# A linear-attention and two-layer MLP kernel: accumulator tiles by bank, another end, another order, diagonals moved to GpSimd, smaller PE tiles in the state update

## The chip, the cores and the metric

One core of a Trainium2 chip. The metric is the device time in microseconds (us) of one execution. All tensors are fp32 in HBM.

## The reference, cut to what matters

```python
# r, k, v, w: (batch 4, heads 8, seq 768, dim 48); u: (8, 48)
for t in range(S):                       # linear attention, a state of 48x48 for each head
    cur = einsum('bhd,bhe->bhde', u * k[t], v[t])
    y[t] = einsum('bhd,bhde->bhe', r[t], state + cur)
    state = w[t][..., None] * state + einsum('bhd,bhe->bhde', k[t], v[t])
x = y as (3072 tokens, 384)
h = x @ w_in                             # 384 -> 2048
g = where(h > 0, h, exp(min(h, 0)) - 1)  # ELU
out = g @ w_out                          # 2048 -> 384
```

## The kernel before, in words

The sequence is cut into 24 **units** and 6 **chunks** of 512 tokens (`NC`, `N`), four units to a chunk. Units 0 to 3 ("whole") hold 128 steps of one batch, units 4 to 23 ("pair") 64 steps of two batches. The weights come packed and are turned on the chip into a high part (fp32r) and a low part; for the first six of the 16 slices of d_ff (`K32 = 6`) chunk 0 uses an fp32 copy instead.

One **unit** is these tasks: loads of w, k and r, v (and of r and k by token, `rk`, where GpSimd makes the diagonal); two scans on VectorE (`e_scan` L430, `g_scan` L440) for the decays; `hats` L445 scales k and r; the diagonal term r*k*u; `spread`, which lays the diagonal out in the tile `am`; on TensorE `score` (L510 transposes, L518 products, and for pair units the first `state_part` at L497); `mask` L528 puts the scores above the diagonal into `am` (VectorE); on TensorE `value` (second `state_part`, then am times v at L497, then the state update kt times v at L553); last the copies `xf`, `xh`, `xl` (L576, L569, L573) that hand 128 columns of x to the MLP and `update` L581 or L583 of the state. A whole unit's first copy is `xf` on ScalarE. The diagonal of units 0 to 7 (`DIAG`) is made by four narrow products on TensorE (`diag_pe` L469) after `r_k_rows` L464 on VectorE; that of units 8 to 23 by two products on GpSimd (L452, L455) and a reduction on VectorE (L459).

One **step** of the MLP is one chunk with one slice f: `g1` makes h by 9 fp32r products of 512 columns (L261; 3 fp32 ones at L257 for the copy), `r1`, `r2` on ScalarE, `stt` on VectorE make the ELU, `gh` on ScalarE and `gl` on VectorE split it, `g2` adds 9 products of 512 columns (L295; L292 for fp32) into the accumulator, three output banks of 512 columns. In chunk 0 the first six steps, in chunk 1 the first four (`FH = (6, 4)`) are done in two halves of 256 columns, so that the first half needs only the chunk's first two units. The accumulator is one tile of three banks (L238). At the end of a chunk ScalarE copies the banks out (`out` L302). The last step of the last chunk is split (L749): bank 0, bank 1, and bank 2 in two halves, each followed by its copy (`end` L308) and its store.

The order of all instructions is made when the kernel is built: `Plan.order` (L115) is a list scheduler over tasks with costs (`COST`), due times (`BEGINS`) and offsets to them (`NUDGE`); each engine then runs its own list in order, with semaphores between engines. Until the time `WARM_END` gaps of the plan on TensorE are filled with products of the identity that nobody reads (`warm` L404).

Of the kernel before, what the change touches and what calls it, by code (L numbers as in the profile page):

```python
# [8 lines left out]
F32 = mybir.dt.float32  # L9
# [27 lines left out]
FH = (6, 4)  # L37
# [23 lines left out]
COST = dict(es=1.2, gs=1.5, pc=0.2, pd=0.9, md=0.2, spa=2.0, spd=0.62, rh=0.62, hat=1.15, rk=0.48, rku=0.48, prk=1.2, prku=1.35, dg=0.5, mk=0.65, mk0=1.2, up=0.48, sc=0.48, xl=0.48,  # L61
            cand=0.56, cv=0.96, wl=0.88, stt=0.62, gl=0.64, fl=0.95, kt=0.53, xh=0.48, a=0.92, sg=2.0, la=0.95, wh=0.82, r1=0.6, r2=0.62, gh=0.62,
            sp=1.95, s=1.6, s0=1.6, s2=1.1, v=1.92, v0=1.6, v2=1.3, g=2.05, g32=2.65, out=0.6)
LAT = 0.06
# [12 lines left out]
DIAG = ["PE"] * 8 + ["POOL"] * 16  # L77
# [6 lines left out]
NUDGE = dict(a={5: -43.25, 8: -22.5, 15: 19.5},  # L84
             cc={5: -29.75, 6: -3.25, 8: 20.75, 11: 8},
             es={1: -8, 3: 25.5, 7: 9.25, 9: 4.75, 16: -17.5},
             g1={2: -0.75, 14: -22, 16: -9.25, 18: -25, 23: -2.25, 24: -6, 25: 30, 34: -0.75, 37: -5.25, 38: -10.75, 42: -10.75, 43: -28.5, 44: 6, 45: 22, 53: 1.75, 57: -5, 60: 8.5, 64: -3.5, 66: -26.25, 68: -19, 76: -26.5, 80: 2.75, 91: 1.5, 104: 4},
             g2={13: 11.5, 18: -40.75, 19: -29, 20: 4, 32: 12.75, 35: 21, 38: 6.25, 47: 2.75, 50: 7.75, 51: 22, 55: 10.25, 61: -25.75, 67: 44.75, 70: 54},
             raw={0: -6},
             rh={0: -1.75, 1: -6.5, 4: 7.5, 8: -2.5, 13: 25.5, 18: -25},  # L90
             s={2: 9, 5: 8, 6: 16.25, 7: 27, 20: 10.5},
             sp={4: -6.5, 5: 1.5, 6: -6.25, 8: 8.75, 10: 15, 11: -0.75, 17: 27.25},
             v={1: 10.5, 2: -32.5, 15: -11.25, 23: -2.5},
             wl={10: 1.25, 11: 8.5, 13: -21})
# [3 lines left out]
class Plan:  # L98
# [16 lines left out]
    def order(self):  # L115
# [31 lines left out]
        for k in ts:  # L147
            if not count[k]:
                ready[ts[k]["eng"]].append(k)
        events, now, order = [], 0.0, []  # L150
        while len(order) < len(ts):
            moved = False
            for e in ready:
# [34 lines left out]
                busy[e] = end  # L188
# [16 lines left out]
            for end, k in sorted(x for x in events if x[0] <= now + 1e-9):  # L205
# [25 lines left out]
def mlp(nc, w_h, w_l, ps_acc, ps_h, ml, gp, po, dst, last=False, w_f=()):  # L231
# [49 lines left out]
    def g2(s, only=None):  # L281
        f, lo, hi = s["f"], s["lo"], s["hi"]
        for m in range(NK):
            parts = 2 if (s["final"] and m == NK - 1 and last) else 1
            for q in range(parts):
                if only not in (None, (m, q)):
                    continue
                s_ = slice(q * (hi - lo) // parts, (q + 1) * (hi - lo) // parts)
                a_ = cut(s, accs()[m]) if s.get("wide") else accs()[m][:, lo + s_.start:lo + s_.stop]
                first, final = s["first"], s["final"] and q == parts - 1  # L290
                if f < len(w_f):
                    nc.tensor.matmul(a_, w_f[f][:, 1, m], fold(s, s["m"][:, s_]), start=first, stop=final)  # L292
                    continue
                for n, (w, g) in enumerate(((w_h, s["gh"]), (w_h, s["gl"]), (w_l, s["gh"]))):
                    nc.tensor.matmul(a_, w[f][:, 1, m], fold(s, g[:, s_]), start=(first and n == 0), stop=(final and n == 2))  # L295
# [8 lines left out]
    def end(m, q):  # L304
        parts = 2 if m == NK - 1 else 1
        s_ = slice(q * N // parts, (q + 1) * N // parts)
        t = po.tile([P, N // parts], F32, tag=("wraw1", "wraw", "wg")[m], name="o", bufs=m or 1)
        (nc.scalar.copy if m + q in (0, 2) else nc.vector.tensor_copy)(t, acc[m][:, s_])  # L308
        (nc.scalar if m + q == 2 else nc.sync).dma_start(dst[m * P:(m + 1) * P, s_], t)
# [4 lines left out]
    return dict(g1=g1, r1=r1, r2=r2, stt=stt, gh=gh, gl=gl, g2=g2, out=out, store=store, end=end)  # L314
# [3 lines left out]
def rwkv_elu_kernel(ctx, tc, wkr, rk, vp, u, uz, gkrw, gv, gu, wraw, out):  # L318
# [69 lines left out]
    def pair(u_):  # L388
        if u_["i"] in SPARE:
            return spare()[:, 0:2]  # L390
        return ps_a.tile([P, 2, N], F32, tag="pa", name="pa", bufs=1)
# [4 lines left out]
    def spare():  # L396
        if not held:
            held.append(ps_acc.tile([P, NK, N], F32, tag="acc", name="acc"))
        return held[0]

    def warm(n):
        pw = spare()[:, 2, 0:P]
# [103 lines left out]
    def score(u_):  # L506
# [6 lines left out]
        u_["pa"] = pa = both[:, :, 0:n].rearrange("t q (p s) -> t q p s", p=NP)  # L513
        for p in range(NP):
            for lo in range(0, C, u_["L"]):
                for q in range(2):
                    rs, ts = slice(64 * q, 64 * q + D), slice(lo, lo + u_["L"])
                    nc.tensor.matmul(pa[ts, 1 - q, p], u_["k"][rs, p, ts], u_["r"][rs, p, ts], start=True, stop=True)  # L518
# [19 lines left out]
    def value(u_):  # L538
# [8 lines left out]
        if u_["last"]:  # L547
            return
# [393 lines left out]
```

## Time and profile before

| what | us |
|---|---|
| median of 3 runs (516.56 to 518.71) | 516.65 |
| the profiled execution, its own time | 519.32 |
| its span, from the first to the last instruction | 517.6 |
| TensorE busy (98%) | 506.4 |
| VectorE busy (65%) | 335.3 |
| ScalarE busy (53%) | 272.9 |
| GpSimd busy (16%) | 85.1 |

The profiled execution lies 1.7 us above its span and 2.7 us above the median. A matmul's row shows a start and a modelled length that runs into the next one; what it costs in a stream is the distance from start to start. An fp32 product is two records, so "x32" at L553 is 16 products.

### The profile page before, as it was taken

To read this page: it belongs to the slowest core of one execution; us is meant where nothing else is said; L and a number is where in the kernel's file an instruction comes from. 1 tells how busy PE (TensorE), PEld (TensorE's weight loads), DVE (VectorE), ACT (ScalarE), POOL (GpSimd) and SP (SyncE) were. 2 spreads that over 40 slices of the span, in tenths; PEclk is the share of its full clock that TensorE was granted. 3 is DMA by queue.
4 is the path that set the end of the run, shared out by engine and by line. 5 is a ranking of instruction groups with operands and counts; after the bars stand their busy time and mean duration, and the time that the engine had idled before them with its cause. 6 is when DMAs were issued, how large, how long until landed. Compare 5 with 4: busy or idle time off the path is not lost.

```text
span 517.6 us, 13928 instructions
## 1 busy us (share of the span) xinstructions
PE 506.4 (98%) x6095; PEld 419.1 (81%) x6095; DVE 335.3 (65%) x475; ACT 272.9 (53%) x534; POOL 85.1 (16%) x85
## 2 busy tenths in 40 slices
PE   8999999999999999999999999999999999999993
PEld 7898888888988888888878888888887877888882
DVE  7799999997789733878524687524788433423331
ACT  4678776857555533656534644425555343634441
POOL 2000000003265500145120034300342100000000
PEclk9799999999999999999999999999999999999997
DMA  8967523402953210533172214312311000100001
GB/s 253 330 230 230 167 83 139 157 3 74 255 155 95 69 53 3 161 107 99 37 229 57 80 50 136 107 59 58 108 49 60 2 3 1 62 0 2 0 1 66
DMA packets 18307, 49.53 MB, mean 96 GB/s; under 512 B 2240, under 2 KB 2624, under 8 KB 18240
## 3 DMA queue, kind: packets, MB, share of 16 engines
q1 hardware_dynamic: 18096, 48.44, 30.3%
q8 instruction: 50, 0.82, 0.7%
q14 instruction: 17, 0.14, 0.1%
q10 hardware_dynamic: 144, 0.13, 0.1%
HBM read 43.85 MB, written 4.72 MB: 94 GB/s over the span
## 4 chain that ended last, share of the span: by engine, by line
PE 96%; ACT 1%; DVE 1%; DMA 1%; issue 0%; DVEq 0%; ACTq 0%
PE acc L295 37%; PE ph L261 37%; PE pa L497 6%; PE acc L292 3%; PE ph L257 3%; PE pa L518 3%; PE pa L553 3%; PE pb L510 2%; PE pb L469 1%; PE acc L404 1%; DMA w<-in_wkr_dram 1%; ACT am L479 0%; PE acc L518 0%; DVE eg L430 0%; DVE eg L440 0%; DVE o L308 0%
## 5 line engine op out<-in xcount | busy, mean ns | idle before, releaser
L271 DVE SCALAR_TENSOR_TENSOR m<-m,ph 128x512 f32<-128x512 f32 (+1 forms) x106 | 66.8, 633 | 89.7 <-ACT m L268 89.3
L265 ACT ACTIVATE m<-ph 128x512 f32<-128x512 f32 (+1 forms) x106 | 59.0, 557 | 99.1 <-PE ph L261 83.7
L295 PE MATMUL acc<-gh,w_l 128*128 128x512 f32 (+1 forms) x283 | 107.5, 380 | 0.0
L261 PE MATMUL ph<-xh,w_l 128*128 128x512 f32 (+1 forms) x282 | 107.4, 381 | 0.0
L279 DVE TENSOR_TENSOR gl<-m,gh 128x512 fp32r<-128x512 f32 (+1 forms) x94 | 65.1, 698 | 47.4 <-ACT gh L275 47.2
L275 ACT CAST gh<-m 128x512 fp32r<-128x512 f32 (+1 forms) x94 | 56.4, 600 | 69.2 <-PE acc L295 40.7
L295 PE MATMUL acc<-gh,w_h 128*128 128x512 f32 (+1 forms) x192 | 74.3, 387 | 0.0
L261 PE MATMUL ph<-xh,w_h 128*128 128x512 f32 (+1 forms) x192 | 74.1, 386 | 0.0
L295 PE MATMUL acc<-gl,w_h 128*128 128x512 f32 (+1 forms) x192 | 72.5, 377 | 0.0
L261 PE MATMUL ph<-xl,w_h 128*128 128x512 f32 (+1 forms) x192 | 72.3, 377 | 0.0
L268 ACT ACTIVATE m<-m 128x512 f32<-128x512 f32 (+1 forms) x106 | 62.5, 591 | 3.0
L295 PEld LDWEIGHTS acc<-gh,w_l 128*128 128x128 f32 x283 | 53.2, 188 | 10.5
L261 PEld LDWEIGHTS ph<-xh,w_l 128*128 128x128 f32 x282 | 53.0, 188 | 10.5
L490 POOL TENSOR_SCALAR_AFFINE_SELECT am<-md 64x512 f32<-64x512 f32 x32 | 32.9, 1027 | 169.9 <-DVE md L459 158.0
L295 PEld LDWEIGHTS acc<-gh,w_h 128*128 128x128 f32 x192 | 36.1, 188 | 7.5
L261 PEld LDWEIGHTS ph<-xh,w_h 128*128 128x128 f32 x192 | 36.1, 188 | 7.1
L261 PEld LDWEIGHTS ph<-xl,w_h 128*128 128x128 f32 x192 | 36.2, 188 | 6.1
L295 PEld LDWEIGHTS acc<-gl,w_h 128*128 128x128 f32 x192 | 36.1, 188 | 6.0
L295 PE MATMUL acc<-gh,w_g 128*128 128x512 f32 (+1 forms) x91 | 36.0, 396 | 1.5 <-DVE o L308 0.8
L261 PE MATMUL ph<-xh,w_g 128*128 128x512 f32 x90 | 36.1, 401 | 0.0
L295 PE MATMUL acc<-gl,w_g 128*128 128x512 f32 (+1 forms) x91 | 35.2, 387 | 0.0
L261 PE MATMUL ph<-xl,w_g 128*128 128x512 f32 x90 | 35.1, 390 | 0.0
(101 smaller groups left out, 718.3 us busy)
## 6 DMA issues: line engine op xcount, KB each, us to landing
wraw<-in_wraw_dram SPq DMA_DIRECT2D x16, 768.0 KB, 5.7
k<-in_wkr_dram SPq DMA_DIRECT2D x24, 448.0 KB, 5.6
v<-in_vp_dram SPq DMA_DIRECT2D x24, 256.0 KB, 6.0
rk<-in_rk_dram SPq DMA_DIRECT2D x16, 384.0 KB, 4.0
w<-in_wkr_dram SPq DMA_DIRECT2D x24, 227.9 KB, 3.9
out_dram<-o SPq DMA_DIRECT2D x17, 256.0 KB, 2.3
wx<-in_wkr_dram SPq DMA_DIRECT2D x8, 227.9 KB, 2.6
ub<-in_u_dram SPq DMA_DIRECT2D x1, 192.0 KB, 6.3
```

The source lines that it names most:

```text
L257: nc.tensor.matmul(ph, w_f[f][:, 0, k], x_[2][:, k], start=(k == 0), stop=(k == NK - 1))
L261: nc.tensor.matmul(ph, w[f][:, 0, k], y[:, k], start=(k == n == 0), stop=(k == NK - 1 and n == 2))
L265: act(s["m"], s["ph"], AF.Relu, scale=-1.0)
L268: act(s["m"], s["m"], AF.Exp, scale=-1.0)
L271: stt_(s["m"], s["m"], -1.0, s["ph"], ALU.add, ALU.max)
L275: nc.scalar.copy(s["gh"], s["m"])
L279: nc.vector.tensor_tensor(s["gl"], s["m"], s["gh"].bitcast(F32), ALU.subtract)
L292: nc.tensor.matmul(a_, w_f[f][:, 1, m], fold(s, s["m"][:, s_]), start=first, stop=final)
L295: nc.tensor.matmul(a_, w[f][:, 1, m], fold(s, g[:, s_]), start=(first and n == 0), stop=(final and n == 2))
L490: nc.gpsimd.affine_select(out=am[rs].rearrange("t q p s -> t (q p) s"), in_=u_["md"][rs].rearrange("t q p -> t (q p)").unsqueeze(2).broadc ...
L497: nc.tensor.matmul(u_["py"][32 * j:32 * j + 32, h, k], l, r, **flags)
L518: nc.tensor.matmul(pa[ts, 1 - q, p], u_["k"][rs, p, ts], u_["r"][rs, p, ts], start=True, stop=True)
```

## The change

1. **One tile per output bank.** `accs` takes three tiles of one bank instead of one of three. A whole unit's scores are two tiles as well, and its `mask` two instructions.
2. **The end.** The third bank is closed two steps early and copied to SBUF (`partial`). The last two steps go to banks 0 and 1 as before; their part of bank 2 goes to other PSUM tiles, 384 columns and then 128 (`CUT`), which VectorE adds to the copy.
3. **No halves in chunk 1** (`FH`).
4. **The diagonals of units 5 to 7 on GpSimd** (`DIAG`), which adds three `rk` loads.
5. **The order searched anew**: other costs, delays and offsets of the plan. Filling products are put only ahead of the first g2.
6. **The state update of pair units by 64x32 tiles** (`WU`) instead of 64x64.

```diff
-FH = (6, 4)
+FH = (6,0)
+WU = 32
+CUT = 384
...
-LAT = 0.06
+LAT, SELF, DRAIN = 0.05, 0.035, 0.19
+NEXT = dict(PE=0.0, DVE=0.084, ACT=0.1, POOL=0.05, SP=0.0)
...
-DIAG = ["PE"] * 8 + ["POOL"] * 16
+DIAG = ['PE']*5+['POOL']*19
...
-NUDGE = dict(a={5: -43.25, 8: -22.5, 15: 19.5},
...
+NUDGE = dict(cc={6: 6.75, 7: -44.75, 10: -20.5, 14: -49.25, 15: -20},
...
     def accs():
         if not acc:
-            t = ps_acc.tile([P, NK, N], F32, tag="acc", name="acc")
-            acc.extend(t[:, m] for m in range(NK))
+            acc.extend(ps_acc.tile([P, N], F32, tag="acc%d" % m, name="acc") for m in range(NK))
         return acc
...
+    def end(m, cols=(0, N), rest=None):
+        t = po.tile([P, cols[1] - cols[0]], F32, tag=("wraw", "wraw1", "wg")[m], name="o", bufs=m or 1)
+        if rest is not None:
+            nc.vector.tensor_tensor(t, rest, box["part"][:, cols[0]:cols[1]], ALU.add)
+        else:
+            (nc.vector.tensor_copy if m else nc.scalar.copy)(t, acc[m])
+        (nc.scalar if cols[1] == N and m == 2 else nc.sync).dma_start(dst[m * P:(m + 1) * P, cols[0]:cols[1]], t)
+
+    def partial():
+        box["part"] = gp.tile([P, N], F32, tag="x2", name="part", bufs=1)
+        nc.scalar.copy(box["part"], acc[2])
...
     def mask(u_):
-        nc.vector.copy_predicated(u_["am"], above[u_["L"]], u_["pa"])
+        if u_["whole"]:
+            for q in range(2):
+                nc.vector.copy_predicated(u_["am"][:, q], above[u_["L"]][:, q], u_["pa"][q])
+        else:
+            nc.vector.copy_predicated(u_["am"], above[u_["L"]], u_["pa"])
...
+        w = 64 if whole else WU
         for p in range(NP):
-            for h, rs in enumerate(rows):
-                for z in range(2):
-                    m = 64 - 16 * z
-                    nc.tensor.matmul(u_["pu"][64 * z:64 * z + m, h, p], kt[rs, p, 64 * z:64 * z + m], v[rs, P * p + 80 * z:P * p + 80 * z + D],
+            for lo in range(0, R2, w):
+                z, m = lo // 64, min(w, R2 - lo)
+                for h, rs in enumerate(rows):
+                    nc.tensor.matmul(u_["pu"][lo:lo + m, h, p], kt[rs, p, lo:lo + m], v[rs, P * p + 80 * z:P * p + 80 * z + D],
                                      start=whole, stop=(whole or p == NP - 1))
...
+                x, y, a, b = prior, s, (0, CUT), (CUT, N)
+                add(("part",), "ACT", K["out"], fns["partial"], [("g2", n - 2)], due=due)
+                add(("g2a", 0), "PE", g * 2 / 3, lambda x=x, g2=g2: g2(x, (0, 1)), [("gl", n - 1), ("g2", n - 2)], due=due)
+                add(("g2a", 1), "PE", g / 3, lambda y=y, g2=g2: g2(y, (0,)), [("gl", n), ("g2a", 0)], due=due)
+                add(("g2a", 2), "PE", g / 3, lambda y=y, g2=g2: g2(y, (1,)), [("g2a", 1)], due=due)
+                add(("g2", n - 1), "PE", g * 2 / 3 * CUT / N, lambda x=x, y=y: rest(x, y, a, lambda: pair(units[-1])[:, 0], "a"), [("g2a", 2)], due=due)
+                add(("g2", n), "PE", g * 2 / 3 * (1 - CUT / N), lambda x=x, y=y: rest(x, y, b, single, "b"), [("g2", n - 1)], due=due)
...
-                if t["began"] < WARM_END:
+                if t["began"] < WARM_END and ("g2", 0) not in done:
```

How the order moves is shown at three places. The first is ScalarE's list around the first products of the MLP: `xf` out of `acc` is unit 1's copy, "am from ident, md" a unit's spread diagonal, "w_f from wraw" a weight slice's first conversion, "m from ph" and "m from m" are `r1` and `r2` of a step. Before:

```order
L576 COPY xf<-acc 128x6x64
L569 CAST xh<-xf 128x6x64
L473 COPY md<-pb 128x8
L596 ACTIVATE w_f<-wraw 128x768
L479 ACTIVATE am<-ident,md 128x128 x8
L265 ACTIVATE m<-ph 128x256
L268 ACTIVATE m<-m 128x256
```

Changed:

```order
L479 COPY md<-pb 128x8
L485 ACTIVATE am<-ident,md 128x128 x8
L611 ACTIVATE w_f<-wraw 128x768
L591 COPY xf<-acc 128x6x64
L584 CAST xh<-xf 128x6x64
L598 COPY st<-acc 112x4x48
L268 ACTIVATE m<-ph 128x256
```

The spread diagonal of unit 2 stood between unit 1's copy and the first step's `r1`; now it stands ahead of both.

The second place is TensorE's list at the end of `value` of a pair unit (unit 4): am times v, then the state update. Before:

```order
L497 MATMUL pa<-am,v 32x64 x32
L553 MATMUL pa<-v,kt 64x48
L553 MATMUL pa<-v,kt 48x48
L553 MATMUL pa<-v,kt 64x48
L553 MATMUL pa<-v,kt 48x48
```

Changed:

```order
L503 MATMUL pa<-am,v 32x64 x32
L568 MATMUL pa<-v,kt 32x48 x6
L568 MATMUL pa<-v,kt 16x48 x2
L568 MATMUL pa<-v,kt 32x48 x6
L568 MATMUL pa<-v,kt 16x48 x2
```

The first row and those below it now have outputs of at most 32 partitions; the products of one update are 32 where they were 16.

The third place is the end of TensorE's list, with the tiles' numbers. Before, the last nine products (`acc_5572` is the whole accumulator):

```order
L295 MATMUL acc_5572<-gh_5948,w_g_1647 128x512
L295 MATMUL acc_5572<-gl_5950,w_g_1647 128x512
L295 MATMUL acc_5572<-gh_5948,w_l_103 128x512
L295 MATMUL acc_5572<-gh_5948,w_g_1647 128x256
L295 MATMUL acc_5572<-gl_5950,w_g_1647 128x256
L295 MATMUL acc_5572<-gh_5948,w_l_103 128x256
L295 MATMUL acc_5572<-gh_5948,w_g_1647 128x256
L295 MATMUL acc_5572<-gl_5950,w_g_1647 128x256
L295 MATMUL acc_5572<-gh_5948,w_l_103 128x256
```

Changed, ten rows from the last of bank 1 on (three more of the last tile follow, with the last step's operands):

```order
L295 MATMUL acc_5757<-gh_6131,w_l_103 128x512
L295 MATMUL pa_6146<-gh_6121,w_g_1616 128x384
L295 MATMUL pa_6146<-gl_6123,w_g_1616 128x384
L295 MATMUL pa_6146<-gh_6121,w_l_103 128x384
L295 MATMUL pa_6146<-gh_6131,w_g_1635 128x384
L295 MATMUL pa_6146<-gl_6135,w_g_1635 128x384
L295 MATMUL pa_6146<-gh_6131,w_l_103 128x384
L295 MATMUL pb_6156<-gh_6121,w_g_1616 128x128
L295 MATMUL pb_6156<-gl_6123,w_g_1616 128x128
L295 MATMUL pb_6156<-gh_6121,w_l_103 128x128
```

Bank 2's products of the last two steps now stand last of all and go to tiles that no copy reads before they are done.

## Rows read from the trace of the kernel before

**Rows 1.** The page's busy time of each engine.

```profile
PE 506.4 (98%) x6095; PEld 419.1 (81%) x6095; DVE 335.3 (65%) x475; ACT 272.9 (53%) x534; POOL 85.1 (16%) x85
```

**Rows 2.** Whom TensorE waited for at the end of the span: us in total, times, the longest.

```profile
PE acc L295 <- DVE o L308: 0.8, 1, 0.8
PE acc L295 <- ACT o L308: 0.7, 1, 0.7
```

**Rows 3.** The timeline of TensorE in the first 50 us: start, us, instruction.

```profile
23.60 2.84 PE L257 MATMUL ph<-xf,w_f 128*128 128x256 f32 x12
26.27 2.84 PE L404 MATMUL acc<-ident 128*128 128x128 f32 x24
28.95 1.46 PE L257 MATMUL ph<-xf,w_f 128*128 128x256 f32 x6
...
47.92 0.67 PE L553 MATMUL pa<-v,kt 128*64 128x48 f32 x16
48.52 1.56 PE L292 MATMUL acc<-m,w_f 128*128 128x256 f32 x6
```

**Rows 4.** The timeline of ScalarE there: unit 1's copy, unit 2's spread diagonal, the first step's r1.

```profile
22.81 0.48 ACT L576 COPY xf<-acc 128x384 f32<-128x384 f32 x1 [1.09 <-PE acc L553]
...
24.65 2.43 ACT L479 ACTIVATE am<-ident,md 128x128 f32<-128x128 f32 x8
26.99 0.36 ACT L265 ACTIVATE m<-ph 128x256 f32<-128x256 f32 x1
```

**Rows 5.** The timeline of TensorE at the diagonal products of one unit and the next instruction.

```profile
110.54 0.95 PE L469 MATMUL pb<-ubd,rkc 112*128 112x2 f32 x8
111.35 0.47 PE L261 MATMUL ph<-xh,w_h 128*128 128x512 f32 x1
```

**Rows 6.** The timeline of TensorE: the first of nine half-width products and the first instruction after them, then the same for nine full-width ones.

```profile
132.17 0.28 PE L261 MATMUL ph<-xh,w_h 128*128 128x256 f32 x1
133.25 0.28 PE L295 MATMUL acc<-gh,w_h 128*128 128x256 f32 x1
...
480.03 0.39 PE L295 MATMUL acc<-gh,w_h 128*128 128x512 f32 x1
482.07 0.39 PE L261 MATMUL ph<-xh,w_g 128*128 128x512 f32 x1
```

**Rows 7.** The timeline of TensorE at `value` of unit 7 (a pair unit): state_part, am times v, the state update, the next step.

```profile
128.21 0.46 PE L497 MATMUL pa<-k,st 48*32 48x64 f32 x32
128.48 0.90 PE L497 MATMUL pa<-am,v 64*32 64x64 f32 x64
129.31 0.68 PE L553 MATMUL pa<-v,kt 64*64 64x48 f32 x32
129.91 0.39 PE L295 MATMUL acc<-gh,w_h 128*128 128x256 f32 x1
```

**Rows 8.** The timeline of TensorE, ScalarE and VectorE at the end; in brackets the engine's idle time before and what ended it.

```profile
507.68 0.39 PE L295 MATMUL acc<-gh,w_l 128*128 128x512 f32 x1
...
508.74 0.39 PE L295 MATMUL acc<-gh,w_g 128*128 128x256 f32 x1 [0.68 <-ACT o L308]
...
509.08 0.27 PE L295 MATMUL acc<-gh,w_l 128*128 128x256 f32 x1
509.45 0.69 DVE L308 COPY o<-acc 128x512 f32<-128x512 f32 x1 [3.40 <-PE acc L295]
510.20 0.38 PE L295 MATMUL acc<-gh,w_g 128*128 128x256 f32 x1 [0.84 <-DVE o L308]
...
510.54 0.28 PE L295 MATMUL acc<-gh,w_l 128*128 128x256 f32 x1
510.90 0.37 ACT L308 COPY o<-acc 128x256 f32<-128x256 f32 x1 [2.21 <-PE acc L295]
...
511.30 0.42 DVE L308 COPY o<-acc 128x256 f32<-128x256 f32 x1 [1.16 <-ACT o L308]
```

**Rows 9.** Stretches of the span: the stretch, its length, then busy us (instructions) of PE, PEld, DVE, ACT and POOL, the granted TensorE clock as a share of full speed, the DMA engines' share, GB/s.

```profile
0.00:26.00 26.00, 23.45 (x217) 20.75 (x218) 19.80 (x30) 13.51 (x37) 3.15 (x13) 0.87 0.95 291
26.00:55.00 29.00, 28.91 (x253) 24.48 (x252) 27.79 (x38) 23.16 (x52) 1.08 (x2) 1.00 0.74 236
55.00:85.00 30.00, 30.00 (x171) 25.51 (x173) 28.68 (x41) 21.91 (x42) 0.00 (x0) 1.00 0.33 116
85.00:116.00 31.00, 31.00 (x558) 25.57 (x549) 29.80 (x42) 21.05 (x37) 0.82 (x1) 1.00 0.27 87
116.00:126.00 10.00, 10.00 (x236) 8.62 (x236) 8.11 (x14) 7.06 (x16) 4.34 (x4) 1.00 0.02 5
```

**Rows 10.** The timeline of VectorE: the mask of unit 7.

```profile
126.06 0.75 DVE L528 COPY_PREDICATED am<-upper_h,pa 128x512 f32<-128x512 uint32 x1 [0.30 <-PE pa L497]
```

**Rows 11.** Groups of instructions by line: busy us, mean ns of one, then idle time before them. VectorE's ELU maximum and its subtraction, GpSimd's two products of the diagonal, and a low weight part on VectorE.

```profile
L271 DVE SCALAR_TENSOR_TENSOR m<-m,ph 128x512 f32<-128x512 f32 (+1 forms) x106 | 66.8, 633 | 89.7 <-ACT m L268 89.3
...
L279 DVE TENSOR_TENSOR gl<-m,gh 128x512 fp32r<-128x512 f32 (+1 forms) x94 | 65.1, 698 | 47.4 <-ACT gh L275 47.2
...
L455 POOL TENSOR_TENSOR rk<-rk,ub 128x384 f32<-128x384 f32 x16 | 21.6, 1358 | 1.1
L452 POOL TENSOR_TENSOR rk<-rk 128x384 f32<-128x384 f32 x16 | 20.6, 1285 | 28.7 <-DMA rk<-in_rk_dram 28.5
...
L630 DVE TENSOR_TENSOR w_l<-w_f,wt 128x768 fp32r<-128x768 f32 x6 | 5.5, 952 | 0.8 <-ACT wt L622 0.8
```

More of the change, by code (lines that the diff above doesn't have):

```diff
@@ L187, in order @@
                 end = now + t["dur"]
-                busy[e] = end
+                busy[e] = end - NEXT[e]
                 if t["lock"]:
@@ L279, in gl, with g2 @@
         nc.vector.tensor_tensor(s["gl"], s["m"], s["gh"].bitcast(F32), ALU.subtract)
-    def g2(s, only=None):
+    def g2(s, banks=(0, 1, 2), cols=None, dst=None, first=None, final=None):
         f, lo, hi = s["f"], s["lo"], s["hi"]
[L283 to L295, printed above, removed]
+        a, b = cols or (0, hi - lo)
+        begin, close = first, final
+        for m in banks:
+            a_ = dst if dst is not None else cut(s, accs()[m]) if s.get("wide") else accs()[m][:, lo + a:lo + b]
+            first, final = s["first"] if begin is None else begin, m in s["final"] if close is None else close
+            if f < len(w_f):
+                nc.tensor.matmul(a_, w_f[f][:, 1, m], fold(s, s["m"][:, a:b]), start=first, stop=final)
+                continue
+            for n, (w, g) in enumerate(((w_h, s["gh"]), (w_h, s["gl"]), (w_l, s["gh"]))):
+                nc.tensor.matmul(a_, w[f][:, 1, m], fold(s, g[:, a:b]), start=(first and n == 0), stop=(final and n == 2))
     box = {}
@@ L302, in out @@
         nc.scalar.copy(box["o"][:, m], acc[m])
[L304 to L309, printed above, removed]
+    def end(m, cols=(0, N), rest=None):
[8 more added lines that the diff above has]
+        nc.scalar.copy(box["part"], acc[2])
     def store(m):
         nc.sync.dma_start(dst[m * P:(m + 1) * P], box["o"][:, m])
-    return dict(g1=g1, r1=r1, r2=r2, stt=stt, gh=gh, gl=gl, g2=g2, out=out, store=store, end=end)
+    return dict(g1=g1, r1=r1, r2=r2, stt=stt, gh=gh, gl=gl, g2=g2, out=out, store=store, end=end, partial=partial)
 @with_exitstack
@@ L389, in pair @@
         if u_["i"] in SPARE:
-            return spare()[:, 0:2]
-        return ps_a.tile([P, 2, N], F32, tag="pa", name="pa", bufs=1)
+            return spare()[0:2]
+        t = ps_a.tile([P, 2, N], F32, tag="pa", name="pa", bufs=1)
+        return [t[:, q] for q in range(2)] if u_["whole"] else t
     def single():
@@ L397, in spare @@
         if not held:
-            held.append(ps_acc.tile([P, NK, N], F32, tag="acc", name="acc"))
-        return held[0]
+            held.extend(ps_acc.tile([P, N], F32, tag="acc%d" % m, name="acc") for m in range(NK))
+        return held
     def warm(n):
-        pw = spare()[:, 2, 0:P]
+        pw = spare()[2][:, 0:P]
         for _ in range(n):
@@ L512, in score @@
         n = NP * u_["L"]
[L513 removed]
+        if u_["whole"]:
+            u_["pa"] = pa = [t[:, 0:n].rearrange("t (p s) -> t p s", p=NP) for t in both]
+        else:
+            u_["pa"] = both[:, :, 0:n].rearrange("t q (p s) -> t q p s", p=NP)
+            pa = [u_["pa"][:, q] for q in range(2)]
         for p in range(NP):
@@ L734, in rwkv_elu_kernel @@
             s, n, part = dict(f=f, lo=lo, hi=hi, wide=(c == 0 and hi - lo < N)), len(seq), (hi - lo) / N
-            s["first"], s["final"] = (f, lo, hi) == steps[c][0], (f, lo, hi) == steps[c][-1]
+            s["first"], final = (f, lo, hi) == steps[c][0], (f, lo, hi) == steps[c][-1]
+            s["final"] = () if not final else range(NK) if c < NC - 1 else (0, 1)
+            if c == NC - 1 and (f, lo, hi) == steps[c][-3]:
+                s["final"] = (2,)
             full = c == 0 and f < K32
```

75 lines of the change are left out of this document (43 added, 32 removed).

## The prediction

> **What bounds the kernel now.** I read the busy times first: TensorE is busy for 506.4 of 517.6 us [rows 1], so only three things can shorten the run: less work on TensorE, fewer waits of TensorE, or an earlier start of its stream. Then the stretches: from 26 to 126 us TensorE has next to no break, and VectorE is busy for 27.79 of 29.00, 28.68 of 30.00 and 29.80 of 31.00 us up to 116 [rows 9]. The reader is to see two engines near their limits there, while VectorE's share of the whole span is 65% [rows 1]: what the change asks of VectorE ahead of 116 us is not free. The early timelines show that TensorE's stream is not real work at first: between 26.27 and 28.95 it runs products that nobody reads [rows 3]. The first step's r1 began only at 26.99, behind unit 2's spread diagonal on ScalarE (24.65, 2.43 us) [rows 4]. The waits and the last timeline show the end: the first half of bank 2 waited for ScalarE's copy of bank 0, the second for VectorE's copy of bank 1 [rows 2, 8], since all banks are one tile.
>
> Against what the result counts: the profiled execution took 519.32 us, its span is 517.6, the median of the runs is 516.65. The sum below is a difference, worked out in the profiled execution; taken from 519.32 it gives 512.8 for a profiled run, and I take it from the median. A difference under 0.5% (2.6 us) counts as none.
>
> **The change, part by part.**
>
> *Diagonals of units 5 to 7.* TensorE loses three groups of four narrow products. One group holds it for 111.35 - 110.54 = 0.81 us [rows 5]: 3 x 0.81 = **-2.4 us**, all in stretches without a break. Three row products on VectorE become three reductions of like size. GpSimd gets six products of about 1.3 us [rows 11]; from 55 to 116 us it was busy for 0.82 us [rows 9], which hides them. The queue of loads gets three more of 384 KB ahead of late weight slices; the DMA engines were at 33% and 27% there [rows 9], so I cost them at nothing. If that cover is gone, a weight slice is late and TensorE waits for it.
>
> *No halves in chunk 1.* Nine half-width products take 133.25 - 132.17 = 1.08 us, 0.120 each; nine full ones 482.07 - 480.03 = 2.04, 0.227 each [rows 6]. Four steps with 18 products each: 72 x (2 x 0.120 - 0.227) = **-1.0 us**.
>
> *State update in 64x32 tiles.* It takes 129.91 - 129.31 = 0.60 us for 32 records of 64x64 [rows 7], in 18 units. The new one has 64 records of the shape that stands in the two rows above it. Their paces: state_part 0.27 us for 32 records, 8.4 ns each, followed by the same tile shape; am times v 0.83 us for 64, 13.0 ns each, followed by another shape [rows 7]. Upper bound, 64 at 13.0 with nothing saved: 0.83 - 0.60 = +0.23 a unit, +4.1 us in all. The lower bound comes from the change of shape: before, one stands between am times v and the update and one behind the update; now only the latter. No row has a change alone; if am times v ran at state_part's 8.4 ns, its 64 records took 0.54 us and the change behind them 0.83 - 0.54 = 0.29. Then the two tasks together were 0.83 + 0.60 = 1.43 us and are 0.54 + 0.54 + 0.29 = 1.37: -0.06 a unit, -1.1 in all; with moving operands of 48 columns, not 64, the update's pace could be 6.3 ns, 0.40 us, and the gain 0.20 a unit, -3.6 us. I take **-1.0 us**: the row nearest to it in shape and in what follows is state_part's.
>
> The Trainium skill, TensorEngine Tiling (Array Packing), section Instruction Overhead, speaks against this part: a matmul has about 60 cycles of overhead, however few columns it has. At 2.4 GHz that is an estimate of 25 ns for each of 16 x 18 = 288 more products, 7.2 us, by which the whole sum would be +1.7. The rows do not bear it out as a fixed price: state_part's 16 products take 0.27 us, 17 ns each [rows 7].
>
> *The end.* The last full product began at 507.68; the next was due 0.23 later, 507.91, and began at 508.74: 0.83 late. The second half was due 0.12 after 509.08 and began at 510.20: 1.00 late [rows 8]. Separate tiles remove both, -1.83. The new last products cost more: 12 full ones, 6 of 384 columns (0.173, between 0.120 and 0.227) and 6 of 128 (0.10; under 0.120) make 4.36 us, against 15 x 0.227 + 6 x 0.12 = 4.12: +0.24. Behind the last product (it ends at 510.82) ScalarE's copy and then VectorE's ended at 511.72, 0.90 later [rows 8]. Now one addition of 128 columns follows; copies of 512 and 256 columns took 0.69 and 0.42, so some 0.28, and 0.08 until it starts: -0.54. Sum **-2.1 us**, bounds -1.5 to -2.4. The copy of bank 2 starts two steps early and is hidden by 24 products.
>
> *The start.* Unit 2's spread diagonal moves ahead of unit 1's copy on ScalarE. The gap of 2.68 us [rows 3] is the most that this can give; least is nothing, since the copy, which the first product needs, now stands behind the spread's 2.43 us. To choose, I followed the new lists of TensorE, ScalarE and VectorE by hand with the durations of the same instructions: unit 3's update ends near 43.8 us with two groups of 1.3 us fewer behind it, against 48.52 [rows 3]; that is a lead of 4.7 - 2.6 = 2.1. I left out hand-overs between engines, so I take **-1.5 us**.
>
> *A new wait.* Without halves chunk 1 can't begin before unit 7 is done. Ahead of unit 7's am times v TensorE now has 45 half-width products less (5.4 us), 9 full ones (2.0) and three diagonal groups (2.4): it is there 9.8 us before 128.48 [rows 7], at 118.7, or 117.2 with the lead. VectorE must have unit 7's mask by then; it began at 126.06 [rows 10]. By the new list eight instructions fewer stand ahead of it, three maxima, three subtractions and two low weight parts, 0.63, 0.70 and 0.95 us each [rows 11], less 0.7 or so for masks now in two pieces and half-width forms: some 4 us. So 122.1; with 10.0 - 8.11 = 1.9 us of idle time that it had from 116 to 126 [rows 9], and the start's lead, down to about 117 to 118. I take a wait of **+1.5 us**, bounds 0 and 4.2 (122.1 plus the mask's 0.75 and a hand-over, 122.9, against 118.7 without a lead). Queued behind the waiting instruction are the update, the last step's g2 and all of chunk 1.
>
> *Separate tiles between chunks, the split masks, GpSimd's spreads:* TensorE waited nowhere between chunks, so nothing is gained there; the mask pieces are counted above.
>
> Sum: -2.4 - 1.0 - 1.0 - 2.1 - 1.5 + 1.5 = **-6.5 us**, so 516.65 - 6.5 = **510.2 us**.
>
> **The rivals.**
>
> *A: each added product pays its slot.* The update runs at 13.0 ns a record with no switch saved, +4.1 instead of -1.0: 510.2 + 5.1 = 515.3 us. For it: am times v has the same 64 rows and tile. Against it: state_part's 8.4 ns. The Trainium skill's rule on overhead, above, is of this kind.
>
> *B: no lead at the start, and VectorE's list is as late as its work allows.* The lead is 0 and the wait 4.2: 510.2 + 1.5 + 2.7 = 514.4 us. For it: VectorE is at 96% there [rows 9]. Against it: part of its idle time before the mask came from the halves' own hand-overs.
>
> *C, slower: GpSimd holds VectorE off.* GpSimd's six new products fall into the stretch in which VectorE has nothing to spare. Each holds VectorE off for its whole length: 3 x (1.36 + 1.29) = 7.9 us [rows 11]. Unit 7's mask then begins at 130.0 instead of 122.1, am times v at 130.8; TensorE, there at 118.7, waits 12.1 us. With no lead: 516.65 - 6.5 + 12.1 = 522.3 us. It decides from a wait of 6.5 + 2.6 = 9.1 us on, unit 7 later than 127.8. Against it: VectorE worked on beside GpSimd from 116 to 126, 8.11 and 4.34 of 10 us [rows 9], and TensorE lost nothing. The Trainium skill, GPSIMD Engine Reference, section Specifications, states that GpSimd's SBUF interfaces are shared with VectorE and that they contend when VectorE reads two SBUF inputs; by it some of C's price is paid, and no row here prices it.
>
> *D: the end's waits stay,* because the copies still hold up the products in some other way: 510.2 + 2.1 = 512.3 us. Little speaks for it; the waits name the copies of one tile [rows 2].
>
> **How the numbers follow.** Forecast 0.70, its own range 506 to 514; A 0.08, B 0.08, C 0.07, D 0.07. Faster by over 0.5% means under 514.1: the forecast and D, 0.77. A and B are within 0.5%: 0.16. C is slower: 0.07. The low end takes in the start's whole gap (-1.2 more), no wait (-1.5) and half of the update's lower bound (-1.3): 506. The high end takes in A: 515.5. What is left out, C, the edge of B and either tail, is about 0.2.
>
> **What the profile after would show.** No wait of TensorE for a copy at the end; the last addition within 0.4 us of the last product; five groups of narrow diagonal products; am times v followed by the update with almost no pause, and the two together under 1.43 us; r1 of the first step right behind its product, with fewer filling products. Wrong would be: TensorE waiting several us for unit 7's mask near 117 to 123 us (B or C), the update above 0.7 us (A), or a wait for a weight slice in chunk 0.

## The result, and the profile after

The changed kernel took 522.9 us (median of 20 runs, 517.7 to 528.7) against 517.0 (20 runs, 515.7 to 521.5): a ratio of 1.0092, 95% interval 1.0068 to 1.0116. The ratio leaves out the five slowest runs of the changed kernel, at a granted clock of 0.975 to 0.981; the two medians alone give 1.0113. It is slower, where 510.2 was forecast. The profiled execution took 524.5 us, its span is 522.8 (before 517.6).

The page of the changed kernel: busy times, the granted clock in 40 slices, the queue that fetches instructions, and the chain that ended last, by engine.

```profile
PE 505.9 (97%) x6572; PEld 415.2 (79%) x6572; DVE 334.2 (64%) x472; ACT 268.7 (51%) x519; POOL 89.0 (17%) x91
...
PEclk8799989999999999999989999999999999999999
...
q8 instruction: 53, 0.87, 0.7%
...
PE 85%; DVE 9%; issue 3%; ACT 1%; DMA 1%; DVEq 0%
```

TensorE is busy for 505.9 us, 0.5 less than in [rows 1], in a span that is 5.2 longer: the work shrank and the idle time grew. 3% of the chain is "issue", time in which an engine waited for nothing that the profile shows. Whom TensorE waited for: us in total, times, the longest.

```profile
PE pa L568 <- issue: 4.7, 3, 2.1
...
PE ph L264 <- DVE m L274: 1.2, 1, 1.2
...
PE pb L652 <- DVE flags L651: 0.9, 1, 0.9
PE pa L503 <- DVE am L540: 0.3, 1, 0.3
```

The copies of [rows 2] are gone. Three waits over 0.5 us are new, and the largest stands in the new state update (L568). The timeline of TensorE at unit 14 shows it (state_part, am times v, the update, then the next step):

```profile
263.36 0.45 PE L503 MATMUL pa<-k,st 48*32 48x64 f32 x32
263.63 0.85 PE L503 MATMUL pa<-am,v 64*32 64x64 f32 x60
...
264.32 0.33 PE L568 MATMUL pa<-v,kt 64*32 64x48 f32 x9
266.77 0.67 PE L568 MATMUL pa<-v,kt 64*16 64x48 f32 x52 [2.12 <-issue]
267.37 0.52 PE L295 MATMUL acc<-gh,w_g 128*128 128x512 f32 x1
267.71 0.60 PE L295 MATMUL acc<-gl,w_g 128*128 128x512 f32 x1
268.11 0.63 PE L295 MATMUL acc<-gh,w_l 128*128 128x512 f32 x1
```

In the middle of the update TensorE starts nothing for over 2 us. Operands are there: the records on either side use the same tiles. The products behind it then follow at 0.40 to 0.43 us instead of 0.227 [rows 6]. Stretches of the same execution, columns as in [rows 9] (granted clock third from the right): the standstill, the stretch behind it, and one behind the wait for VectorE at 71 us.

```profile
264.45:266.77 2.32, 0.20 (x19) 0.06 (x6) 0.69 (x1) 0.28 (x1) 0.66 (x1) 1.00 1.04 312
267.73:271.14 3.41, 3.41 (x10) 2.64 (x9) 1.62 (x3) 0.76 (x2) 1.16 (x1) 0.50 0.06 18
73.17:76.58 3.41, 3.41 (x9) 2.64 (x8) 3.41 (x6) 1.50 (x5) 0.00 (x0) 0.50 0.87 323
```

Behind two of the waits the granted clock is 0.50 (1.2 GHz) for 3.41 us; half of that, 1.7 us, is what each costs. What stood at the start of the standstill is seen in the DMA view of 264.20 to 264.40 us:

```profile
q8 instruction: 1, 0.02, 30.0%
```

That packet, 16 KB of instructions, began at 264.27; TensorE stopped at 264.45 and went on 2.50 us after the fetch began. The other two: fetch at 355.01, stopped for 0.90 us from 356.27, on at 2.16; fetch at 364.51, stopped for 2.09 us from 364.85, on at 2.43 (times behind the start of the fetch). Where in the program they stand can be counted: in the instructions that the trace records for TensorE (13,211, weight loads and products nearly all), the three stops are behind numbers 7361, 9921 and 10433, each 193 beyond a multiple of 256. With 53 fetches, one fetch stands for some 250 of them. So TensorE stops at the same place of a block each time, and goes on 2.2 to 2.5 us after a fetch began.

Undisturbed, the two tasks together (am times v and the update) take 1.40 us in 15 of 18 units, against 1.44 before; unit 4, from the start of am times v to the next step:

```profile
88.60 0.85 PE L503 MATMUL pa<-am,v 64*32 64x64 f32 x60
...
89.99 0.50 PE L295 MATMUL acc<-gh,w_h 128*128 128x512 f32 x1
```

**The sum closes.** From the first fp32r step to the start of the last product the kernel before took 446.2 us (64.33 to 510.54), the changed one 451.1 (64.87 to 515.98): +4.9. The two first products, before and changed:

```profile
64.33 0.58 PE L261 MATMUL ph<-xh,w_h 128*128 128x512 f32 x1
...
64.87 0.58 PE L264 MATMUL ph<-xh,w_h 128*128 128x512 f32 x1
```

The forecast's terms there, without the mask's wait (there was none), are -6.0: diagonals -2.4, halves -1.0, update -1.0, end -1.6. Add the standstills (2.3 + 0.9 + 2.1 = 5.3), the wait for VectorE at 71 us (1.2), that for the flags (0.9) and two stretches at half clock (3.4): +4.8. Ahead of that step +0.5, where -1.5 was forecast; behind the last product -0.2, where -0.5 was.

**What one trace does not show.** The record has the granted clock of every run. In the changed kernel's 20 runs the time goes with it: 517.7 to 518.7 us in the three runs at 0.991 to 0.996, 520.6 to 523.0 in the eight at 0.983 to 0.990, 524.2 to 528.7 in the nine below. Its median clock is 0.983; that of the kernel before is 0.992 in the 118 runs beside the experiments, of which those at 0.991 to 0.996 took 516.6 us (median). So most of the 5.9 us between the medians goes with the clock: 2 x 0.009 x 523 = 9.4 us more at half clock, an estimate of 4.7 us. Where in a run the half clock lies, only the profiled one tells.

### The profile page after: what moved, and what is told of

Read it like the earlier page. It is cut to its first block, busy times and chain, and to the rows that moved or that the text cites. A ratio compares the mean times of both kernels' runs of the same rounds, so it can differ in the third digit from the quotient of the medians.

```text
span 522.8 us, 14865 instructions
## 1 busy us (share of the span) xinstructions
PE 505.9 (97%) x6572; PEld 415.2 (79%) x6572; DVE 334.2 (64%) x472; ACT 268.7 (51%) x519; POOL 89.0 (17%) x91
## 4 chain that ended last, share of the span: by engine, by line
PE 85%; DVE 9%; issue 3%; ACT 1%; DMA 1%; DVEq 0%
PE acc L295 35%; PE ph L264 34%; PE pa L503 6%; PE pa L528 3%; PE pa L568 2%; DVE eg L436 2%; PE pb L516 2%; DVE k L451 1%; DVE m L274 1%; PE ph L260 1%; PE acc L292 1%; DVE eg L446 1%; DVE gl L282 1%; DMA w<-in_wkr_dram 1%; PE acc L410 1%
## 5 line engine op out<-in xcount | busy, mean ns | idle before, releaser
L264 PE MATMUL ph<-xh,w_l 128*128 128x512 f32 x270 | 106.1, 393 | 0.0
L295 PE MATMUL acc<-gh,w_l 128*128 128x512 f32 x268 | 105.2, 393 | 0.0
L282 DVE TENSOR_TENSOR gl<-m,gh 128x512 fp32r<-128x512 f32 x90 | 65.5, 731 | 39.7 <-ACT gh L278 39.2
L278 ACT CAST gh<-m 128x512 fp32r<-128x512 f32 x90 | 55.7, 619 | 53.0 <-DVE m L274 32.9
L264 PE MATMUL ph<-xh,w_h 128*128 128x512 f32 x180 | 72.1, 400 | 1.2 <-DVE m L274 1.2
L295 PE MATMUL acc<-gh,w_h 128*128 128x512 f32 x180 | 71.9, 399 | 0.0
L264 PE MATMUL ph<-xl,w_h 128*128 128x512 f32 x180 | 70.7, 393 | 0.0
L295 PE MATMUL acc<-gl,w_h 128*128 128x512 f32 x180 | 70.3, 391 | 0.0
L295 PE MATMUL acc<-gh,w_g 128*128 128x512 f32 x88 | 36.0, 409 | 0.0
L295 PE MATMUL acc<-gl,w_g 128*128 128x512 f32 x88 | 35.2, 400 | 0.0
```

Source lines behind the costliest of these rows:

```text
L264: nc.tensor.matmul(ph, w[f][:, 0, k], y[:, k], start=(k == n == 0), stop=(k == NK - 1 and n == 2))
L278: nc.scalar.copy(s["gh"], s["m"])
L282: nc.vector.tensor_tensor(s["gl"], s["m"], s["gh"].bitcast(F32), ALU.subtract)
L295: nc.tensor.matmul(a_, w[f][:, 1, m], fold(s, g[:, a:b]), start=(first and n == 0), stop=(final and n == 2))
```

## Experiments

**Theory 1**: TensorE's instructions run out; the 32 more records of an update make a run of 160 small ones in 1.7 us, faster than they are fetched. **Theory 2**: the new order is at fault. **Theory 3**: GpSimd's products hold VectorE up. **Theories 4 and 5** concern the half clock. Each time is the median of that kernel's own runs; each ratio is to the kernel before on the same chip, with its 95% interval in brackets. A standstill is given from start to start, a wait as idle time.

### e1: the changed kernel, update in 64x64 tiles

```diff
-WU = 32
+WU = 64
```

> The changed kernel with the state update back in 64x64 tiles (WU = 64), the order untouched. Theory 1 (TensorE's instructions run out): the 32 more records of each pair unit's update let TensorE empty its store of instructions; in the changed kernel's trace three updates stood still for 2.35, 0.90 and 2.13 us with nothing to wait for, and one was followed by 3.4 us at half clock that cost 1.69, 7.1 us together. Without the extra records these go, and the update costs its 1.1 us more: 522.9 - 7.1 + 1.1 = 516.9 us, 515.5 to 518.5; the trace shows no update that stands still for over 0.5 us. Theory 2 (the new order is at fault: a wait for VectorE at 71 us with a half clock behind it, the guard's wait at 453): the time stays at 521 to 524 us.

Measured 517.4 us, ratio 1.001 (0.998 to 1.004). The waits:

```profile
PE ph L264 <- DVE m L274: 1.2, 1, 1.2
PE pb L652 <- DVE flags L651: 0.9, 1, 0.9
PE pa L503 <- issue: 0.7, 1, 0.7
```

The update stands still no more; 5.5 us come back by the medians (4.2 by the two ratios), as theory 1 said. One standstill of 0.88 us is left, now in am times v. The new order's two other waits stay.

### e2: the kernel before, update in 64x32 tiles

```diff
-            for h, rs in enumerate(rows):
-                for z in range(2):
-                    m = 64 - 16 * z
+            for lo in range(0, R2, w):
+                z, m = lo // 64, min(w, R2 - lo)
+                for h, rs in enumerate(rows):
```

> The kernel before with only the state update of pair units by 64x32 tiles, the order untouched. Theory 1: updates stand still here too, by chance of where the fetches fall, and some are followed by a half clock: 517.0 - 1.1 + 3 to 7 = 519 to 523 us. Theory 2: only the gain is there, 517.0 - 1.1 = 515.9 us (515.4 to 516.5), and no update stands still for over 0.5 us.

Measured 519.0 us, 1.0046 (1.0029 to 1.0063), at theory 1's lower end.

```profile
PE ph L262 <- issue: 1.5, 2, 1.4
PE pa L555 <- issue: 1.0, 1, 1.0
```

The larger of the two stands not in an update but in a product of 512 columns right behind one, 1.88 us from start to start, and ends 2.4 us after a fetch began. So 64x32 tiles alone make the old order slower. The four medians: old order 516.6 (64x64) and 519.0 (64x32), new order 517.4 and 522.9. The tiles cost 2.4 us in one order and 5.5 in the other (4.2 by the ratios); the new order with 64x64 tiles is no faster than the old, so theory 2 keeps a part: its two waits and what they bring.

### e3: the kernel before with one tile per bank and the new end

The edit is parts 1 and 2 of the change; halves, diagonals, tiles and the list of tasks up to the end are as before.

> The kernel before with only one tile per output bank, split masks of the whole units and the new end; order up to the end, halves, diagonals and the update as before. Both theories: the end's waits go as forecast, 517.0 - 2.1 = 514.9 us (514.4 to 515.6). If the end's gain is not real, 517.0.

Measured 514.7 us, 0.9967 (0.995 to 0.998): the term of the end, forecast -2.1, measured -1.8. In the profiled executions the stretch from the first fp32r step to the start of the last product is 2.3 us shorter (443.9 against 446.2) and the end behind it 0.4 longer. The waits of [rows 2] are gone; its only waits:

```profile
PE acc L410 <- POOL ident masks.py:199: 1.6, 1, 1.6
PE pb L475 <- DVE rkc L470: 0.9, 1, 0.9
PE pb L516 <- ACT md L479: 0.3, 1, 0.3
```

### e4: half of the update left out

```diff
-        for p in range(NP):
+        for p in range(NP) if whole else (0, NP - 1):
```

> The changed kernel with the middle two of the four head pairs of the state update left out (the states of those heads are then not updated): the update keeps its 64x32 tiles and has 32 records a pair unit again, as many as before the change. Theory 1 (number of records): updates stand still no more, 522.9 - 7.1 - 18 x 0.27 = 511 us (509 to 513). Rival 1b (the 64x32 shape behind am times v is what stalls, however many records): the stalls stay, 522.9 - 4.9 = 518 us (516 to 520).

Measured 513.2 us, 0.992 (0.989 to 0.995). With half the records the issue waits fall from 4.7 to 0.8 us, so the shape alone is not it; two standstills of 0.6 us are left. 511 was expected; the four of its 12 runs at a granted clock of 0.994 or more took 508.5 to 510.4, the others, at 0.988 or less, 512.6 to 515.6.

### e5: the guard's product later

```diff
+    def guard_late():
+        pf = single()
         nc.tensor.matmul(pf[0:1, 0:NU + 1], ones_c, flags, start=True, stop=True)
```

It is called four product tasks behind `guard`, whose flags stay where they were; 64x64 tiles, the order otherwise the changed kernel's, task by task. This is the base of e6 to e8, e11, e12 and e15.

> The changed kernel with the update in 64x64 tiles and the guard's product on TensorE moved three steps' halves later than VectorE's flags (the order is otherwise the changed kernel's, task by task). Without the wait of 0.9 us for the flags near 450 us the time is 1.1 us below that of the 64x64 kernel, 517.4 - 1.1 = 516.3 us. If TensorE would have waited for something else there, 517.4.

Measured 516.1 us, 0.996 (0.993 to 0.999): the flags' wait is gone. The median is 1.3 us lower than in e1, but the intervals touch, so these runs do not price the wait. Two standstills are there in the profiled execution (520.2 us, with 17 us of half clock at the start): 1.39 us at unit 5, 1.15 at unit 18 (the later texts on record say 19). Moving one product shifted what lies in which block.

### e6: unit 5's diagonal back on TensorE

```diff
-DIAG = ['PE']*5+['POOL']*19
+DIAG = ['PE']*6+['POOL']*18
```

> As the kernel with the later guard product, and the diagonal of unit 5 back on TensorE: four narrow products, a row product on VectorE and a copy on ScalarE in place of two products on GpSimd and a reduction on VectorE. Theory 3 (GpSimd's products of unit 5 slow VectorE's scaling of k from 1.22 to 2.03 and 2.07 us, so that VectorE frees the buffer of h 1.2 us late near 70 us, and the half clock behind that wait costs up to 1.7): both scalings take 1.22 us, the wait and the half clock are gone, 516.3 - 1.2 - (0 to 1.7) + 0.8 = 514.2 to 515.9 us. Rival 3b (VectorE is late by its own list): the scalings may be faster but the wait of over 1 us stays, and the time is 516.3 + 0.8 = 517.1 us.

Measured 517.6 us, 0.9995 (0.997 to 1.002). In the changed kernel, GpSimd's products of unit 5 and VectorE's scaling of k:

```profile
62.84 2.15 POOL L458 TENSOR_TENSOR rk<-rk 128x384 f32<-128x384 f32 x1 [25.17 <-DMA rk<-in_rk_dram]
64.05 2.03 DVE L451 TENSOR_TENSOR k<-k,eg 112x1024 f32<-112x1024 f32 x1
67.17 2.86 POOL L461 TENSOR_TENSOR rk<-rk,ub 128x384 f32<-128x384 f32 x1 [2.18 <-DMA ub<-in_u_dram]
...
69.04 2.07 DVE L451 TENSOR_TENSOR k<-k,eg 112x1024 f32<-112x1024 f32 x1
```

In e6:

```profile
63.36 1.23 DVE L509 TENSOR_TENSOR k<-k,eg 112x1024 f32<-112x1024 f32 x1
67.55 1.21 DVE L509 TENSOR_TENSOR k<-k,eg 112x1024 f32<-112x1024 f32 x1
```

The mechanism of theory 3 holds: both scalings are back at 1.2 us, and no wait over 0.3 us is left near 70. The plan forbids such pairs at one time, but its lock sets only the order of lists; on the chip GpSimd starts when its load lands. The Trainium skill, GPSIMD Engine Reference, section Specifications, says that GpSimd's SBUF interfaces are shared with VectorE, with contention when VectorE's instruction has two SBUF inputs. This scaling has two (k and eg), and these rows agree. It does not hit every time: in e5 the scaling at 66.82 us took 1.22 us inside a GpSimd product that took 2.96. The time did not fall, against the expectation: standstills of 1.60 us (unit 5) and 1.50 (unit 18) stand in this kernel.

### e7: the wait filled

```diff
+        for _ in range(s.get("pad", 0)):      # 5 for the step ahead of the wait
+            nc.tensor.matmul(ph, w_h[f][:, 0, 0], xh[:, 0], start=True, stop=True)
```

> As the kernel with the later guard product, with five products that nobody reads ahead of the step before the wait near 70 us: 1.13 us of TensorE work where it would wait 1.2 us. Theory 4 (the half clock follows the wait): the stretch of half clock behind it is gone at no cost, and the time falls by up to 1.7 us, 516.3 - 1.5 = 514.8 us. Rival 4b (the half clock there has another cause): the stretch stays and the time is 516.3 us or more.

Measured 516.9 us, 0.998 (0.995 to 1.001); no half clock near 70, but e5 without the filling had none there either in its profile. Inconclusive. Six profiles have a wait there of 1.05 to 1.2 us; the half clock follows in the changed kernel, e1 and e9 and does not in e10, e11 and e12, so the wait alone does not decide it.

### e8: all diagonals of units 5 to 7 on TensorE

```diff
-DIAG = ['PE']*5+['POOL']*19
+DIAG = ['PE']*8+['POOL']*16
```

> As the kernel with unit 5's diagonal on TensorE, and those of units 6 and 7 on TensorE too, as in the kernel before. By the forecast's term each group costs TensorE 0.8 us that nothing hides: 1.6 us more than with unit 5 alone, so 515.8 to 517.5 us. Rival (GpSimd's products of units 6 and 7 cost VectorE, and so TensorE, as much as they save): the same time as with unit 5 alone, or less.

Measured 516.7 us, 0.9996 (0.998 to 1.002): within the expected band, but below e6, so the medians price nothing. From the first fp32r step to the last product e5, e6 and e8 took 443.8, 445.5 and 445.3 us; less their standstills (2.5, 3.1 and 1.9) that is 441.2, 442.4 and 443.5. So three groups cost some 2.2 us in these three profiles, near the forecast's 2.4, hidden by standstills that differ by over 1 us.

### e9 and e10: nothing but a shift

```diff
+    def shift():
+        for _ in range(32):                   # e9; 16 in e10
+            nc.tensor.matmul(spare()[2][0:32, 0:32], ident[0:64, 0:32], ident[0:64, 0:32], start=True, stop=True)
```

It runs at the start; everything else, 64x32 tiles too, is the changed kernel task by task.

> The changed kernel, its order task by task, with 32 small products that nobody reads (64 records, 0.5 us at most, before the first real product, while TensorE waits for the first operands). They do nothing but shift every later instruction of TensorE by 64 records against the 16 KB blocks in which its instructions are fetched. Theory 1 in its sharper form (an update stands still where a fetch begins inside the run of small products, until 2.2 to 2.6 us after the fetch began): the three updates that stood still at 264, 356 and 365 us do so no more, or for other lengths, and others may; the sum of the stalls is anything from 0 to 5 us, the time 516 to 523 us, and each stall over 0.5 us ends 2.1 to 2.8 us after a fetch began. Rival 1c (the number of small products in a short stretch decides by itself): the same three updates stall for 2.3, 0.9 and 2.1 us again and the time is 522.9 us.

> As the last one with 16 small products, a shift by 32 records. Theory 1: another set of stalls than with 0 and with 64. Rival 1c: the same three stalls, 522.9 us.

e9 took 526.4 us (6 runs, one of them, 982.6, not explained; 525.2 without it), 1.016 (1.012 to 1.020), slower than expected; e10 523.5, 1.012 (1.009 to 1.015). e10's waits, and one place in its timeline:

```profile
PE pa L630 <- issue: 6.5, 5, 1.8
PE pa L565 <- issue: 1.8, 2, 1.1
```

```profile
96.27 0.85 PE L565 MATMUL pa<-am,v 64*32 64x64 f32 x60
...
96.96 0.73 PE L630 MATMUL pa<-v,kt 64*32 64x48 f32 x56
99.46 0.27 PE L630 MATMUL pa<-v,kt 64*32 64x48 f32 x5 [1.77 <-issue]
```

Both medians are above what I expected at most (523). The three old places, units 14, 18 and 19, lost their 2.3, 0.9 and 2.1 us (left are 1.3 at unit 14 and 0.9 at 19 in e10, 0.5 at 18 in e9); new ones stand at units 5, 8, 9 and 20 in e9, at 5, 6, 7 and 21 in e10, where all seven sum up to 9.7 us. In the 13 kernels with standstills I matched each one over 0.5 us between two records of am times v, `state_part` or the update behind 60 us with the fetches of 16 KB: 30, and all end 2.2 to 2.8 us after a fetch began. Five more, of 1.2 to 2.4 us, stand in products of 512 columns within 3 us behind an update (e2, three in e9, e12) and end 2.4 to 2.6 us after a fetch. Counted as above, all 35 begin 192 or 193 instructions beyond a multiple of 256. Other transfers do not set the length: in e10 the DMA engines were busy at 2% between fetch and end at 111 us (2.37 us) and at 95% at 264 us (2.42). Where the block's edge falls in the program decides, not the unit: rival 1c fails. Nor is it the clock: the runs of e9 (without the 982.6) and e10 stand at a median of 0.994 and 0.996, against 0.983 for the changed kernel, and take longer.

### e11, e12 and e15: the shift with 64x64 tiles

> The kernel with 64x64 updates and the later guard product, shifted by 64 records. Unshifted it stalled at unit 5 (1.39 us) and unit 19 (1.15 us) and took 516.1 us. Theory 1: these two stalls change or go; with none left 513.6 us (516.1 - 2.5), at worst 518. Rival 1c: the same two stalls and 516.1 us.

> The kernel with 64x64 updates and the later guard product, shifted by 32 records. Theory 1: another set of stalls, 513.6 to 518 us. Rival 1c: the same two stalls and 516.1 us.

> The kernel with 64x64 updates, the later guard product and the changed order, shifted by 96 records. Theory 1: a third set of stalls (with 0 two, of 1.4 and 1.2 us; with 64 one of 0.9; with 32 two, of 2.0 and 1.1); 513.0 us with none, 517 with two. If the time stays at 515.4 whatever the stalls, they are not what decides.

(e15 has 24 small products, a shift by 48 records; the text on record says 96.) Measured 515.5, 515.4 and 515.9 us; ratios 0.998 (0.996 to 1.001), 0.997 (0.994 to 0.999) and 0.999 (0.996 to 1.001). Standstills in e11: 0.89 us; in e12: 1.08, and 2.43 among the products of 512 columns behind unit 14's update; in e15: 1.55. Each shift has another set, as expected; but the medians do not follow them from shift to shift, and runs of one kernel spread by 4 to 6 us. The profiled executions do follow: from the first fp32r step to the start of the last product they took 442.7, 447.0 and 444.1 us; less standstills, waits and half the stretch of half clock (e12) 440.7, 440.8 and 441.1. Treated alike, e1 leaves 440.9, e9 441.1, e10 440.5 and the changed kernel 440.3. The forecast's terms ask for 446.2 - 6.0 = 440.2 with 64x32 tiles and 441.2 with 64x64.

### e13 and e14: the start

The kernel before, and e3's, with 16 such products at the start.

> The kernel before with 16 small products that nobody reads ahead of its first filling products (32 records, 1.8 us, while TensorE waits for operands), nothing else changed. In the four kernels with such products the stretch of half clock between 8 and 21 us is missing, in the others of both orders it lasts 3.4 to 17 us. Theory 5 (that stretch hangs on what TensorE does in its first microseconds, and takes 1.2 us of the time for each 3.4 us): it is gone here too and the first fp32r step begins near 61.5 us instead of 64.3; the time is 516.9 - 1.5 = 515.4 us, shift or no shift. Rival 5b (only the changed order's start does this): the stretch stays and the time is 516.9 us.

> The kernel before with one tile per bank and the new end, and the same 16 small products at the start: the parts that were shown to gain, without the rest of the change. 514.7 - 1.0 = 513.7 us (513.0 to 514.7); the shift by 32 records may bring a stall of up to 2 us, since no order was chosen for it.

Measured 517.3 us, 1.002 (1.000 to 1.004), and 515.3, 0.999 (0.997 to 1.001). The stretch from 8 to 21 us in the kernel before and in e13:

```profile
8.00:21.00 13.00, 12.47 (x124) 10.65 (x123) 10.67 (x13) 8.16 (x25) 0.00 (x0) 0.74 1.03 321
```

```profile
8.00:21.00 13.00, 11.75 (x180) 10.26 (x179) 11.94 (x15) 9.13 (x27) 0.00 (x0) 1.00 1.03 341
```

The half clock at the start is gone (0.74 to 1.00), and so it is in the profiled executions of all seven kernels with such products; of the ten without, only e1 has none there (against my text). But neither median fell, and four of e13's 12 runs stand at 0.988 to 0.991, some 3 to 6 us more of half clock, place unknown. So theory 5 is right on what moves the stretch in the profiled executions and wrong on its price. By the median the fastest complete version is e3; the whole intervals of e3, e5 and e12 lie below the kernel before, none of the three by over 0.5%.

## Why the prediction was wrong

- **The step that failed is the state update**, "I take -1.0 us". Its pace was right: 1.40 us for the two tasks against 1.44 is 18 x 0.04 = -0.7. The Trainium skill's rule on overhead per product (TensorEngine Tiling (Array Packing), Instruction Overhead) did not decide either; by the estimate of 25 ns worked out from it the two tasks would have been slower by 0.4 us a unit, and they were faster by 0.04. I priced records by the duration of records and never asked what supplies them. 32 more in a run of 128 made the supply fail, 5.3 us in the profiled execution, and a stretch at half clock behind one of the three (1.7). The Trainium skill, Runtime: NRT & Kernel Launch, section Instruction fetch mechanics, says that code comes in blocks of 16 KiB and that crossing into one is mostly hidden; the packets here have that size, and crossing cost up to 2.3 us. A sign stood in the trace of before: in unit 15 the two tasks took 1.85 us instead of 1.44, the update's records standing still for 0.42 us until 2.8 us after a fetch began.
- **The clock was no term of the forecast.** By the runs' granted clock it took an estimate of 4.7 us; the profiled execution shows 3.4 of it behind two waits and 1.7 in a longer stretch at the start. The runs at 0.991 to 0.996 are 7.5 to 8.5 us above 510.2; the standstills (5.3) and the two waits (2.1) are 7.4.
- **A wait "for unit 7's mask", +1.5: nearly none came.** The mask began at 120.74; the weight loads for `value` waited 0.41 us for it, which the product still running hid: `value` began 0.37 us behind that product's start, at unit 14 it is 0.32. TensorE was itself some 3 us later than I had worked out, but that was not what saved it: in e1, where it came at 117.8, the wait was as short. VectorE was late elsewhere, at 71 us, by rival C's mechanism on a small scale: 1.2 us, and a half clock behind it. I had hidden GpSimd's products behind VectorE's work; the cover was wrong where VectorE had no idle time [rows 9].
- **The guard** was not in my steps. In the new order its product stands right behind its flags' turn on VectorE: 0.9 us in the profile, gone in e5.
- **The start, -1.5:** the first fp32r step began at 64.87 instead of 64.33. The spread diagonal moved as described, but the profiled execution had 10.2 us of half clock at the start against 6.8. Without any half clock there, the step began at 61.0 to 64.2 in the new order (e1, e9 to e12, e15) and at 62.3 and 61.3 in the old (e13, e14): no lead of 1.5 us is seen at equal clock.
- **The end, -2.1:** right in the main, -1.8 (e3). Here the last addition began 0.3 us behind the start of the last product:

```profile
515.98 0.27 PE L295 MATMUL pb<-gh,w_l 128*128 128x128 f32 x1
...
516.29 0.29 DVE L307 TENSOR_TENSOR o<-pb,part 128x128 f32<-128x128 f32 x1
```

- **Diagonals and halves, -2.4 and -1.0:** the sum above closes with them to 0.1 us, and that of six more kernels to 1 us; alone, only the diagonals were tried (e8).
- The rivals: A (1.66 us for the two tasks, measured 1.40) and D did not come. B's missing lead came, its wait did not. C's mechanism came at a tenth of its price; that its 522.3 us lies near the measured 522.9 is luck.
- Still open: why the first fp32r step moves by 3 us among kernels of the new order without half clock there, and why some waits and standstills have a half clock behind them and others not. Argued, not shown: that the new order, which packs units closer (am times v of units 17 to 19 within 16 us of each other, before within 32), makes standstills likelier.

## What to carry to other kernels

Count instructions, not only their durations: in and behind runs of small products of 8 to 13 ns a record TensorE stood still at places 256 instructions apart, and a gap that ends some 2.4 us after a fetch on the instruction queue, put down to "issue", is the sign. Where such runs exist, any edit, even one that adds a product at the start, moves the gaps, so two versions a per cent apart are compared by their profiles with the gaps counted and by the granted clock of their runs, not by times alone. And a lock in a plan that makes lists is not a lock on the chip: an engine off the critical path starts when its load lands.

## What the hardware showed that I had not expected

- Standstills of up to 2.4 us from start to start in the middle of TensorE's list, each at the same place modulo 256 recorded instructions and each ending 2.2 to 2.8 us after a 16 KB instruction fetch began, with 49 to 54 fetches in a run. Some stand in large products just behind a run of small ones.
- GpSimd's two products of the diagonal took 2.15 and 2.86 us beside VectorE where other units' take as little as 1.02, and slowed VectorE's from 1.22 to 2.03 and 2.07.
- In the profiled executions of seven kernels with 16 to 32 small products at 1.6 us, a stretch of 3.4 to 17 us of half clock is missing that nine of the ten others have, from 8 to 15 us into the span; the medians of e13 and e14 did not follow.
- Of 20 runs of one kernel the time ranged from 517.7 us at a granted clock of 0.993 to 528.7 at 0.975.
